# A decode block: softmax in groups between key heads, a fixed VectorE order, and a re-ordered value stage and tail

## Chip, cores, metric

One core of one Trainium2 chip. The metric is device time in microseconds (us). Most quoted times are medians of several executions; a "span" is that of the one profiled execution, from its first to its last instruction, and is 1.7 to 2.1 us shorter than the same execution's time. "Stream" below means the transfers from HBM (the main memory of the chip) into SBUF (the working memory of the core) as a whole. To "evict" a result is to copy it out of the accumulator in which TensorE left it; here VectorE does this.

## The reference, cut to what matters

One token passes an attention block and a feed-forward block, each with a layer norm modulated by a condition `c`. Attention reads the last 4096 keys and values of 32 heads of 192 elements, and each key and value is used once.

```python
mod = (silu(c) @ w_mod)                        # sa, ca, ga, sb, cb, gb: six vectors of 640
h = layernorm(x) * (1 + ca) + sa
q = h @ wq                                     # 32 heads x 192
p = softmax(q @ k.T * 192 ** -0.5)             # per head, 4096 keys
x = x + ga * ((p @ v) @ wo)
h = layernorm(x) * (1 + cb) + sb
x = x + gb * (mish(h @ w1 + b1) @ w2)
```

K and V are 50.3 MB each; with the weights the kernel reads 125.24 MB.

## The kernel before

All large transfers come from one queue (SyncE). K heads, V heads and the weights of the second half share a pool `kv` of six buffers, so a transfer is issued only when the buffer of six tiles earlier is free. For K, VectorE multiplies a head by the query, TensorE adds up the products in twelve matmuls with an identity, VectorE reduces the rest.

```python
kv = ctx.enter_context(tc.tile_pool(name="kv", bufs=6))
pp = ctx.enter_context(tc.tile_pool(name="pp", bufs=2))
...
def k_reduce(h):
    nc.vector.tensor_reduce(out=S[:, h, :], in_=accs.pop(h)[:], axis=AX.X, op=ALU.add)
...
for h in range(H):                                  # K stage; wo comes in six pieces between
    ...
    kt = kv.tile([P, T, Dh], BF, tag="kv")
    nc.sync.dma_start(out=kt[:], in_=A_k_cache[0, h, Sk - W:Sk, :].rearrange("(p t) d -> p t d", p=P))
    ...                                             # at h == 2: both later parts of w_mod
    nc.vector.tensor_tensor(out=prod[:], in0=kt[:], in1=qbc[:, h:h + 1, :].to_broadcast([P, T, Dh]), op=ALU.mult)
    for d1 in range(ND1):
        nc.tensor.matmul(acc[:], lhsT=ident[:], rhs=prod[:, :, d1 * D2:(d1 + 1) * D2], ...)
    accs[h] = acc
    if h >= 1:
        k_reduce(h - 1)
k_reduce(H - 1)

m1 = ...                                            # one softmax for all 32 heads: maximum,
...                                                 # transpose, subtract, Exp, sum, reciprocal
nc.vector.tensor_tensor(out=Pm[:], in0=E[:], in1=rinv[:].unsqueeze(2).to_broadcast([P, H, T]), op=ALU.mult)

for i in range(NPAIR):                              # V stage, two heads at a time
    for hh in range(2):
        nc.sync.dma_start(out=vt[:], in_=A_v_cache[0, h, Sk - W:Sk, :].rearrange("(p t) d -> p (t d)", p=P))
        for t0 in range(0, T, G):
            nc.tensor.matmul(acc[:], lhsT=Pm[:, h, t0:t0 + G], rhs=vt[:, t0 * Dh:(t0 + G) * Dh], ...)
        nc.vector.tensor_copy(out=osb[:, :, hh, :], in_=acc[:])
    ...                                             # six tiny matmuls transpose osb into pt, copied to oT
    if i >= 1:
        wo_stage(i - 1)                             # fifteen matmuls with wo, added to attn
... # loads of w1 (two pieces) and w2 (two pieces), last wo_stage, norm, ph = w1 part, mish, py = w2 part, out
```

Of the kernel before, what the change touches and what calls it, by code (L numbers as in the profile page):

```python
# [7 lines left out]
BF = mybir.dt.bfloat16  # L8
F32 = mybir.dt.float32
ALU = mybir.AluOpType  # L10
AX = mybir.AxisListType
ACT = mybir.ActivationFunctionType
# [4 lines left out]
def kernel(  # L17
# [15 lines left out]
    nc = tc.nc  # L33
    P = 128
    D = A_x.shape[2]
# [5 lines left out]
    KC = D // P  # L41
# [46 lines left out]
    onesf = const.tile([P, P], F32)  # L88
    nc.gpsimd.memset(onesf[:], 1.0)
    epsb = const.tile([P, 1], F32)  # L90
    nc.gpsimd.memset(epsb[:], EPS)
# [71 lines left out]

    S = const.tile([P, H, T], F32)
    modB = const.tile([P, 4 * KC], F32)
    accs = {}

    def k_reduce(h):
        nc.vector.tensor_reduce(out=S[:, h, :], in_=accs.pop(h)[:], axis=AX.X, op=ALU.add)  # L169

# [4 lines left out]
    MODB_AT = 2  # L175
    wmbs = []
    for h in range(H):
        if h in WO_AT:
            b_ = WO_AT[h]
            nc.sync.dma_start(out=wo_t[:, b_ * JB:(b_ + 1) * JB, :],  # L180
                              in_=A_wo[b_ * JB * P:(b_ + 1) * JB * P, :].rearrange("(j p) n -> p j n", p=P))
        kt = kv.tile([P, T, Dh], BF, tag="kv")
        nc.sync.dma_start(out=kt[:], in_=A_k_cache[0, h, Sk - W:Sk, :].rearrange("(p t) d -> p t d", p=P))
        if h == MODB_AT:
            for b_ in range(2):
                wmb = kv.tile([P, KC, 2 * D], BF, tag="kv")
                nc.sync.dma_start(out=wmb[:], in_=w_mod[:, (2 + 2 * b_) * D:(4 + 2 * b_) * D].rearrange("(k p) n -> p k n", p=P))
                wmbs.append(wmb)
        prod = pp.tile([P, T, Dh], BF, tag="prod")
        nc.vector.tensor_tensor(out=prod[:], in0=kt[:], in1=qbc[:, h:h + 1, :].to_broadcast([P, T, Dh]),  # L190
                                op=ALU.mult)
        acc = psA.tile([P, T, D2], F32, tag="A")
        for d1 in range(ND1):
            nc.tensor.matmul(acc[:], lhsT=ident[:], rhs=prod[:, :, d1 * D2:(d1 + 1) * D2],  # L194
                             start=(d1 == 0), stop=(d1 == ND1 - 1))
        accs[h] = acc
        if h >= 1:
            k_reduce(h - 1)
        if h == MODB_AT + 1:
            pmb = psC.tile([P, 4 * KC], F32, tag="C")  # L200
            for j in range(4 * KC):
                wmb = wmbs[j // (2 * KC)]
                jo = (j % (2 * KC)) * P
                for k in range(KC):
                    nc.tensor.matmul(pmb[:, j:j + 1], lhsT=wmb[:, k, jo:jo + P], rhs=scT[:, k:k + 1],
                                     start=(k == 0), stop=(k == KC - 1))
            nc.scalar.copy(out=modB[:], in_=pmb[:])
    k_reduce(H - 1)

    m1 = small.tile([P, H], F32)  # L210
    nc.vector.tensor_reduce(out=m1[:], in_=S[:], axis=AX.X, op=ALU.max)  # L211
    pmT = psC.tile([H, P], F32, tag="C")
    nc.tensor.transpose(pmT[:], m1[:], identf[:])
    gm = small.tile([H, 1], F32)
    nc.vector.tensor_reduce(out=gm[:], in_=pmT[:], axis=AX.X, op=ALU.max)
    dg = small.tile([H, H], F32)
    nc.vector.tensor_scalar_mul(out=dg[:], in0=identf[0:H, 0:H], scalar1=gm[:])
    pgb = psC.tile([P, H], F32, tag="C")
    nc.tensor.matmul(pgb[:], lhsT=onesf[0:H, :], rhs=dg[:], start=True, stop=True)
    nc.vector.tensor_tensor(out=S[:], in0=S[:], in1=pgb[:].unsqueeze(2).to_broadcast([P, H, T]),  # L220
                            op=ALU.subtract)
    E = const.tile([P, H, T], F32)
    nc.scalar.activation(out=E[:], in_=S[:], func=ACT.Exp, scale=SCALE)  # L223
    rs = small.tile([P, H], F32)
    nc.vector.tensor_reduce(out=rs[:], in_=E[:], axis=AX.X, op=ALU.add)  # L225
    pss = psC.tile([P, H], F32, tag="C")
    nc.tensor.matmul(pss[:], lhsT=onesf[:], rhs=rs[:], start=True, stop=True)
    rinv = small.tile([P, H], F32)
    nc.vector.reciprocal(out=rinv[:], in_=pss[:])
    Pm = const.tile([P, H, T], BF)  # L230
    nc.vector.tensor_tensor(out=Pm[:], in0=E[:], in1=rinv[:].unsqueeze(2).to_broadcast([P, H, T]),  # L231
                            op=ALU.mult)

    attn = const.tile([P, KC], F32)
    oTs = {}

    def wo_stage(i):
        oT = oTs.pop(i)
        pa = psC.tile([P, KC], F32, tag="C")
        for n in range(KC):  # L240
            for ci in range(3):
                nc.tensor.matmul(pa[:, n:n + 1], lhsT=wo_t[:, 3 * i + ci, n * P:(n + 1) * P],  # L242
                                 rhs=oT[:, ci:ci + 1], start=(ci == 0), stop=(ci == 2))
        if i == 0:
            nc.vector.tensor_copy(out=attn[:], in_=pa[:])
        else:
            nc.vector.tensor_tensor(out=attn[:], in0=attn[:], in1=pa[:], op=ALU.add)  # L247

    G = 2
    for i in range(NPAIR):  # L250
        osb = small.tile([G, G, 2, Dh], BF, tag="osb")
        for hh in range(2):
            h = 2 * i + hh
            vt = kv.tile([P, T * Dh], BF, tag="kv")
            nc.sync.dma_start(out=vt[:], in_=A_v_cache[0, h, Sk - W:Sk, :].rearrange("(p t) d -> p (t d)", p=P))
            acc = psB.tile([G, G, Dh], F32, tag="B")
            for t0 in range(0, T, G):
                nc.tensor.matmul(acc[:], lhsT=Pm[:, h, t0:t0 + G], rhs=vt[:, t0 * Dh:(t0 + G) * Dh],  # L258
                                 start=(t0 == 0), stop=(t0 == T - G))
            nc.vector.tensor_copy(out=osb[:, :, hh, :], in_=acc[:])  # L260
        pt = psC.tile([P, 3], F32, tag="C")
        for ci in range(3):
            for g in range(G):
                nc.tensor.matmul(pt[:, ci:ci + 1],  # L264
                                 lhsT=osb[:, g].rearrange("k a d -> k (a d)")[:, ci * P:(ci + 1) * P],
                                 rhs=ident[0:G, g:g + 1], start=(g == 0), stop=(g == G - 1))
        oT = small.tile([P, 3], BF, tag="oT")
        nc.vector.tensor_copy(out=oT[:], in_=pt[:])  # L268
        oTs[i] = oT
        if i >= 1:  # L270
            wo_stage(i - 1)
    w1a = kv.tile([P, 3, F], BF, tag="kv")
# [4 lines left out]
    for b_ in range(2):  # L277
        w = kv.tile([P, FC // 2, D], BF, tag="kv")
        nc.sync.dma_start(out=w[:], in_=B_w2[b_ * (F // 2):(b_ + 1) * (F // 2), :].rearrange("(f p) n -> p f n", p=P))
        w2_t.append(w)  # L280
    wo_stage(NPAIR - 1)

    x1 = const.tile([P, KC], F32)
    nc.vector.tensor_tensor(out=x1[:], in0=attn[:], in1=modB[:, 0:KC], op=ALU.mult)
    nc.vector.tensor_tensor(out=x1[:], in0=x1[:], in1=xT[:], op=ALU.add)
    xn2 = layernorm_T(x1[:], "l2")
    h2a = small.tile([P, KC], F32)
    nc.vector.scalar_tensor_tensor(out=h2a[:], in0=modB[:, 2 * KC:3 * KC], scalar=1.0, in1=xn2[:],
                                   op0=ALU.add, op1=ALU.mult)
    h2T = small.tile([P, KC], BF)  # L290
    nc.vector.tensor_tensor(out=h2T[:], in0=h2a[:], in1=modB[:, KC:2 * KC], op=ALU.add)  # L291

    ph = psC.tile([P, FC], F32, tag="C")
    nc.tensor.matmul(ph[:], lhsT=ident[:], rhs=b1T, start=True, stop=False)
    for f in range(FC):
        for k in range(KC):
            wt = w1a[:, k, f * P:(f + 1) * P] if k < 3 else w1b[:, k - 3, f * P:(f + 1) * P]
            nc.tensor.matmul(ph[:, f:f + 1], lhsT=wt, rhs=h2T[:, k:k + 1],  # L298
                             start=False, stop=(f == FC - 1 and k == KC - 1))
    hc = small.tile([P, FC], F32)  # L300
    nc.vector.tensor_scalar(out=hc[:], in0=ph[:], scalar1=20.0, scalar2=-80.0, op0=ALU.min, op1=ALU.max)
    u = small.tile([P, FC], F32)
# [7 lines left out]
    actT = small.tile([P, FC], BF)  # L310
    nc.vector.tensor_tensor(out=actT[:], in0=nn_[:], in1=ph[:], op=ALU.mult)

    py = psC.tile([P, KC], F32, tag="C")
    for n in range(KC):
        for f in range(FC):
            wt = w2_t[f // (FC // 2)]
            nc.tensor.matmul(py[:, n:n + 1], lhsT=wt[:, f % (FC // 2), n * P:(n + 1) * P], rhs=actT[:, f:f + 1],  # L317
                             start=(f == 0), stop=(f == FC - 1))
    x2 = small.tile([P, KC], F32)
    nc.vector.tensor_tensor(out=x2[:], in0=py[:], in1=modB[:, 3 * KC:4 * KC], op=ALU.mult)  # L320
    x2b = small.tile([P, KC], BF)
    nc.vector.tensor_tensor(out=x2b[:], in0=x2[:], in1=x1[:], op=ALU.add)
    pxo = psC.tile([KC, P], BF, tag="C")
    nc.tensor.transpose(pxo[:], x2b[:], ident[:])
    xo = small.tile([KC, P], BF)
# [32 lines left out]
```

## Time and profile before

| | before |
|---|---|
| time, median of 16 executions (lowest to highest) | 334.83 us (330.14 to 336.43) |
| profiled execution, and its span | 335.64, 333.9 us |
| DMA bytes, mean rate over the span | 125.47 MB, 376 GB/s |
| PE (TensorE), DVE (VectorE), ACT (ScalarE) busy | 70%, 49%, 2% |

At the time of the prediction the first four of these executions were known (median 335.51). Two of the sixteen are near 330.1 and the rest above 333; the profiled one lies near the median.

How to read it: the DMA row gives the busy tenths of the transfer engines in 40 slices, the row under it the GB/s. In a table of windows a line is a stretch of time with the busy time of PE, PE weight loads, DVE, ACT, POOL (counts of instructions in brackets), then TensorE's granted clock (as a share of full speed), the DMA share and GB/s. In a line of waits the three numbers are the idle time in all, how often, and the longest. In a timeline a line is start, length, engine, source line, operation, result<-inputs, and in square brackets how long the engine stood idle before and what ended that. The lines themselves are in the prediction.

### The profile page before, as it was taken

What the parts mean: (1) busy time and instruction counts of PE and PEld (TensorE: products, weight loads), DVE (VectorE), ACT (ScalarE), POOL (GpSimd) and SP (SyncE); (2) the same over time, 40 slices, a digit from 0 to 9 for tenths busy, and PEclk for the clock granted to TensorE, in tenths of its full rate; (3) what the DMA queues carried; (4) which work ended last, traced back from release to release, by engine and by line L of the source; (5) the groups of instructions that cost most, each with busy time, mean ns of one, the idle gap of its engine ahead of it and who ended that gap; (6) DMA issues with size and microseconds to landing.
All of it is one profiled execution on the core that took longest, in us unless ns stands there. A gap on an engine that the chain in (4) does not pass through costs nothing.

```text
span 333.9 us, 3612 instructions
## 1 busy us (share of the span) xinstructions
PE 234.8 (70%) x1572; PEld 110.1 (33%) x1574; DVE 164.8 (49%) x179; ACT 7.4 (2%) x15; POOL 1.3 (0%) x10
## 2 busy tenths in 40 slices
PE   0495684587587586675774928997888878888844
PEld 0342251233233132232231313554444444443423
DVE  1222858589787887797797552212111121112231
ACT  1021000000000000000000010000000000000000
POOL 1000000000000000000000000000000000000000
PEclk9999795879989699699599675999999999999985
DMA  7999999999999999999999950999999999999900
GB/s 271 410 410 428 403 420 398 427 417 410 424 396 428 425 399 428 413 407 428 399 426 427 425 229 16 402 430 428 423 423 425 425 429 423 424 422 410 304 0 2
DMA packets 21702, 125.47 MB, mean 376 GB/s; under 512 B 1335, under 2 KB 9015, under 8 KB 13495
## 3 DMA queue, kind: packets, MB, share of 16 engines
q1 hardware_dynamic: 21642, 125.25, 91.8%
q8 instruction: 12, 0.20, 0.2%
q14 instruction: 4, 0.02, 0.0%
q10 hardware_dynamic: 44, 0.01, 0.0%
HBM read 125.24 MB, written 0.00 MB: 375 GB/s over the span
## 4 chain that ended last, share of the span: by engine, by line
PE 49%; DVE 29%; DMA 15%; issue 6%; ACT 1%; SPq 0%; DVEq 0%
PE acc L258 27%; DVE prod L190 19%; PE acc L194 16%; DMA kt<-in_A_k_cache_dram 10%; DMA wq_t<-in_A_wq_dram 5%; DVE osb L260 5%; DVE S L169 2%; PE pa L242 2%; PE pt L264 2%; PE py L317 1%; PE ph L298 1%; DVE Pm L231 0%; DVE S L220 0%; DVE m L211 0%; DVE rs L225 0%
## 5 line engine op out<-in xcount | busy, mean ns | idle before, releaser
L194 PE MATMUL acc<-prod,ident 128*128 128x512 bf16 x384 | 106.2, 439 | 51.1 <-DVE prod L190 51.1
L190 DVE TENSOR_TENSOR prod<-kt,qbc 128x6144 bf16<-128x6144 bf16 x32 | 106.6, 3350 | 3.2 <-DMA kt<-in_A_k_cache_dram 3.2
L258 PE MATMUL acc<-vt,Pm 128*2 128x384 bf16 x512 | 90.8, 332 | 1.7 <-DVE Pm L231 1.7
L194 PEld LDWEIGHTS <-ident 128*128 128x128 bf16 x384 | 42.0, 109 | 115.0 <-issue 83.9
L260 DVE CAST osb<-acc 2x384 bf16<-2x384 f32 x32 | 17.5, 546 | 80.9 <-PE acc L258 80.9
L258 PEld LDWEIGHTS <-Pm 128*2 128x2 bf16 x512 | 41.1, 85 | 39.7 <-issue 3.1
L169 DVE TENSOR_REDUCE S<-acc 128x32 f32<-128x512 f32 x32 | 22.0, 688 | 31.2 <-PE acc L194 31.2
L157 PE MATMUL pq<-wq_t,hrep 128*128 128x512 bf16 x58 | 15.6, 428 | 6.6 <-DMA wq_t<-in_A_wq_dram 6.3
L264 PE MATMUL pt<-ident,osb 2*128 2x1 bf16 x96 | 7.1, 163 | 16.7 <-DVE osb L260 16.6
L264 PEld LDWEIGHTS <-osb 2*128 2x128 bf16 x96 | 4.3, 92 | 28.8 <-DVE osb L260 27.3
L162 DVE CAST qbc<-pq 128x512 bf16<-128x512 f32 x6 | 4.2, 692 | 17.3 <-PE pq L157 17.3
L157 PEld LDWEIGHTS <-hrep 128*128 128x128 bf16 x60 | 6.4, 108 | 15.4 <-issue 5.7
L242 PE MATMUL pa<-oT,wo_t 128*128 128x1 bf16 x240 | 8.4, 164 | 0.3 <-DVE oT L268 0.3
L247 DVE TENSOR_TENSOR attn<-attn,pa 128x5 f32<-128x5 f32 x15 | 2.4, 161 | 10.4 <-PE pa L242 10.4
L242 PEld LDWEIGHTS <-wo_t 128*128 128x128 bf16 x240 | 7.1, 96 | 0.6 <-issue 0.2
L268 DVE CAST oT<-pt 128x3 bf16<-128x3 f32 x16 | 2.6, 165 | 6.0 <-PE pt L264 5.9
L117 PE MATMUL pvT<-ident,rows 22*128 22x22 bf16 x1 | 0.2, 174 | 7.0 <-DMA rows<-in_B_b_dram 7.0
L223 ACT ACTIVATE E<-S 128x1024 f32<-128x1024 f32 x1 | 1.1, 1056 | 146.7 <-DVE S L220 146.7
L160 ACT CAST qbc<-pq 128x512 bf16<-128x512 f32 x6 | 3.5, 586 | 18.4 <-PE pq L157 18.4
L119 DVE COPY vecT<-pvT 128x22 bf16<-128x22 bf16 x1 | 0.2, 169 | 7.2 <-PE pvT L117 7.2
L108 ACT ACTIVATE lnv<-var,epsb 128x1 f32<-128x1 f32 x2 | 0.6, 294 | 127.8 <-DVE var L106 127.8
L298 PE MATMUL ph<-h2T,w1a 128*128 128x1 bf16 x36 | 1.7, 165 | 2.3 <-DVE h2T L291 2.3
(77 smaller groups left out, 38.6 us busy)
## 6 DMA issues: line engine op xcount, KB each, us to landing
kt<-in_A_k_cache_dram SPq DMA_DIRECT2D x32, 1536.0 KB, 19.2
vt<-in_A_v_cache_dram SPq DMA_DIRECT2D x32, 1536.0 KB, 10.6
wq_t<-in_A_wq_dram SPq DMA_DIRECT2D x3, 2560.0 KB, 18.8
wo_t<-in_A_wo_dram SPq DMA_DIRECT2D x6, 1280.0 KB, 20.7
wmb<-in_w_mod_dram SPq DMA_DIRECT2D x2, 1600.0 KB
w<-in_B_w_dram SPq DMA_DIRECT2D x2, 960.0 KB
wma<-in_w_mod_dram SPq DMA_DIRECT2D x1, 1600.0 KB, 7.0
w1a<-in_B_w_dram SPq DMA_DIRECT2D x1, 1152.0 KB, 9.1
```

The costliest lines, as they stand in the source:

```text
L157: nc.tensor.matmul(pq[:], lhsT=hrep[:, k, :], rhs=wq_t[:, k, n * 512:(n + 1) * 512], start=(k == 0), stop=(k == KC - 1))
L160: nc.scalar.copy(out=qflat[:, n * 512:(n + 1) * 512], in_=pq[:])
L162: nc.vector.tensor_copy(out=qflat[:, n * 512:(n + 1) * 512], in_=pq[:])
L169: nc.vector.tensor_reduce(out=S[:, h, :], in_=accs.pop(h)[:], axis=AX.X, op=ALU.add)
L190: nc.vector.tensor_tensor(out=prod[:], in0=kt[:], in1=qbc[:, h:h + 1, :].to_broadcast([P, T, Dh]), op=ALU.mult)
L194: nc.tensor.matmul(acc[:], lhsT=ident[:], rhs=prod[:, :, d1 * D2:(d1 + 1) * D2], start=(d1 == 0), stop=(d1 == ND1 - 1))
L242: nc.tensor.matmul(pa[:, n:n + 1], lhsT=wo_t[:, 3 * i + ci, n * P:(n + 1) * P], rhs=oT[:, ci:ci + 1], start=(ci == 0), stop=(ci == 2))
L258: nc.tensor.matmul(acc[:], lhsT=Pm[:, h, t0:t0 + G], rhs=vt[:, t0 * Dh:(t0 + G) * Dh], start=(t0 == 0), stop=(t0 == T - G))
L260: nc.vector.tensor_copy(out=osb[:, :, hh, :], in_=acc[:])
L264: nc.tensor.matmul(pt[:, ci:ci + 1], lhsT=osb[:, g].rearrange("k a d -> k (a d)")[:, ci * P:(ci + 1) * P], rhs=ident[0:G, g:g + 1], start= ...
L298: nc.tensor.matmul(ph[:, f:f + 1], lhsT=wt, rhs=h2T[:, k:k + 1], start=False, stop=(f == FC - 1 and k == KC - 1))
L317: nc.tensor.matmul(py[:, n:n + 1], lhsT=wt[:, f % (FC // 2), n * P:(n + 1) * P], rhs=actT[:, f:f + 1], start=(f == 0), stop=(f == FC - 1))
```

## The change

Its intent: take the softmax chain out of the way of the V stage by doing heads 0 to 7, 8 to 15, 16 to 23 between later K heads; fix VectorE's order in the K stage (product of head h+1, then the reduce of head h); take stalls out of TensorE's V stage (transposes behind the next head's matmuls, normalisation folded into the eviction, `wo` on VectorE for 14 of 16 pairs); move the last third of `w_mod` behind V; and shorten the tail's chain. The core of the diff:

```diff
     def k_reduce(h):
-        nc.vector.tensor_reduce(out=S[:, h, :], ...)
+        with tc.issue_after(prods[min(h + 1, H - 1)].ins):
+            reds[h] = nc.vector.tensor_reduce(out=S[:, h, :], ...)
+    GH = 8
+    def softmax_steps(g):          # four steps for heads g*8 .. g*8+7
+        s1: max over the free axis, transpose          s2: max, diagonal, matmul broadcast
+        s3: negm on ScalarE, then per head
+            nc.scalar.activation(out=Pm[:, h_, :], in_=S[:, h_, :], func=ACT.Exp, scale=SCALE,
+                                 bias=negm[:, j:j + 1], accum_out=rs[:, h_:h_ + 1])
+        s4: matmul with ones over rs, reciprocal into rinv
...
-            for b_ in range(2): ... wmb ...            # both later parts of w_mod in the K stage
+            wmb1 = kv.tile(...)                        # one of them
-        nc.vector.tensor_tensor(out=prod[:], ...)
+        with tc.issue_after(reds[h - 2].ins) if h >= 2 else nullcontext():
+            prods[h] = nc.vector.tensor_tensor(out=prod[:], ...)
+        if pending:
+            pending.pop(0)()
+            if h % GH == 0:
+                pending.extend(softmax_steps(h // GH - 1))
...                                                    # V stage
-            nc.vector.tensor_copy(out=osb[:, :, hh, :], in_=acc[:])
-        pt = ... transposes ...; wo_stage(i - 1)
+            nc.vector.tensor_scalar_mul(out=osb[:, :, hh, :], in0=acc[:], scalar1=rinv[0:G, h:h + 1])
+            if hh == 0 and i >= 1:
+                with tc.issue_after(last.ins):
+                    pts[i - 1] = transposes(osbs.pop(i - 1))
+                wo_dve(i - 1)                          # three scalar_tensor_tensor; the last two pairs: wo_pe
...                                                    # the last V pair is loaded in halves
+    wmb2 = kv.tile(...); nc.sync.dma_start(out=wmb2[:], in_=w_mod[:, 4 * D:6 * D]...)   # behind V
...                                                    # tail: norm folded into two columns of ph, sums by accum_out,
                                                       # the residual added inside the last matmul
```

## The prediction

> **What bounds the kernel now.** I read the 40-slice view first, then a table of windows, then the waits and the timeline at the places where the DMA row falls off.
>
> ```profile
> DMA  7999999999999999999999950999999999999900
> GB/s 271 410 410 428 403 420 398 427 417 410 424 396 428 425 399 428 413 407 428 399 426 427 425 229 16 402 430 428 423 423 425 425 429 423 424 422 410 304 0 2
> ```
>
> A slice is 8.35 us. The DMA engines are full almost everywhere, at 400 to 430 GB/s, so the memory stream is the bound. It is broken twice: about slices 23 and 24, and at the end. The kernel reads 125.24 MB. The windows (microseconds from the start; the last two columns are the DMA share and GB/s) say how long it is broken:
>
> ```profile
> 0.00:196.00 196.00, 127.13 (x598) 53.31 (x600) 134.56 (x91) 5.68 (x11) 1.27 (x10) 0.88 1.01 410
> 198.00:207.00 9.00, 5.74 (x19) 2.50 (x20) 2.80 (x3) 0.24 (x1) 0.00 (x0) 0.50 0.00 0
> 225.00:300.00 75.00, 62.20 (x528) 32.01 (x527) 14.18 (x40) 0.00 (x0) 0.00 (x0) 1.00 1.01 424
> 316.00:317.00 1.00, 0.36 (x10) 0.29 (x10) 0.55 (x1) 0.00 (x0) 0.00 (x0) 1.00 0.94 343
> 317.00:318.00 1.00, 1.00 (x20) 0.67 (x17) 0.16 (x1) 0.00 (x0) 0.00 (x0) 1.00 0.05 15
> ```
>
> By summing windows, 80.4 MB (all K, weights so far, and exactly six V heads, one per buffer of the pool) have landed by 196.4; then nothing moves until 208.2: a **hole of 11.8 us**. The last byte of all comes at 317.05, so the end of 333.9 lies **16.9 us** behind it. The timeline shows the cause of the hole:
>
> ```profile
> 192.44 0.69 DVE L169 TENSOR_REDUCE S<-acc 128x32 f32<-128x512 f32 x1 [2.32 <-PE acc L194]
> 200.61 1.22 DVE L231 TENSOR_TENSOR Pm<-E,rinv 128x1024 bf16<-128x1024 f32 x1
> 201.89 7.94 PE L258 MATMUL acc<-vt,Pm 128*2 128x384 bf16 x32 [1.71 <-DVE Pm L231]
> ```
>
> The softmax of all 32 heads is a serial chain between the last K reduce and the first V matmul; no V buffer comes free in it. In the V stage the pace is set by TensorE all the same:
>
> ```profile
> SPq L255 <- PE acc L258: 99.4, 26, 19.4
> PE pt L264 <- DVE osb L260: 16.6, 26, 0.6
> 225.90 0.20 PE L264 MATMUL pt<-ident,osb 2*128 2x1 bf16 x2 [0.64 <-DVE osb L260]
> 226.03 0.53 PE L242 MATMUL pa<-oT,wo_t 128*128 128x1 bf16 x15
> ```
>
> The queue that issues V waits on the matmuls that free buffers, and TensorE itself stands 0.64 us per head behind the eviction of its own result. A pair of heads takes 7.57 us (230.06 back to 222.50), 2 x 1.573 MB in that time being 416 GB/s, a little under the 424 the stream still manages by working off a backlog.
>
> **What the Trainium skill says.** "DMA: Bandwidth & Descriptors", section "Where 436 GB/s comes from", gives 435 GB/s as the ceiling of the ports into SBUF and about 358 as the share of HBM for a core. The trace shows 424 to 428, so here the first figure is the near one and no headroom in rate is left. The same page, "Anatomy of one DMA", says that the semaphore waits for the last byte to be confirmed. The trace agrees: 1.638 MB and the first 2.621 MB of wq have passed at about 13.2, and the matmul that waits for them starts at 14.18, so 1.0 us. "Perfetto Trace Analysis", "Optimization Strategy", suggests interleaving regimes that are bound by different engines; the hole is such a border. "ScalarE: Activation LUTs", "What ACT_TABLE_LOAD costs", gives an activation with a pointer bias about 280 ns + 0.833 ns per element; the trace has 294 ns for 128x1 (lnv), so I take 0.31 us for each new 128x32 exponential.
>
> **The change, part by part.** No byte is added or taken. So I follow the stream.
>
> (1) *Softmax in four groups of eight heads.* Three groups go between heads of the K stage. In the instruction order of the changed build, the first V matmul stands directly behind the last K matmul and waits for its DMA alone; the last group's small steps lie between V matmuls. The 11.8 us hole should vanish. Added on VectorE per group: a 128x256 maximum (about a quarter of the 1.22 us, plus overhead, 0.35), gm 0.25, dg 0.2, a reciprocal 0.2: 1.0 us. Removed: four 128x1024 passes of 1.22 us, all from the hole. On ScalarE 8 x 0.31 = 2.5 us per group; in groups 1 and 3 the sum over partitions follows at once on TensorE, which then stands some 3 us. Five buffers ahead, about 18 us, absorb that.
>
> (2) *Fixed order prod(h+1), reduce(h).* Before, VectorE idled 31.2 us in 16 of the reduces, behind TensorE. Two instructions that don't wait repeat each 3.87 us (prod 3.35 and reduce 0.69, overlapped a little). Five heads: 19.4 + 0.6 softmax = 20.0 us. The stream needs 5 x 1.573/0.428 = 18.4 and a wo piece at about 357 GB/s (from the dips to 402) 3.7: 22.1 us. So VectorE keeps up, and K ends with its transfers: 69.3 MB, near 170, + 8 us for the last products. Nothing of this shortens the stream itself; it keeps the backlog small.
>
> (3) *V stage.* Transposes go behind the next head's matmuls, and wo moves to VectorE for 14 pairs. TensorE per pair: 2 x 2.71 + 0.45 = 5.9 us. VectorE: 2 x 0.55 + 0.17 + 3 x 0.82 (estimate: the 128x640 f32 cast took 0.819) = 3.7 us. The stream: 3.146/0.424 = 7.4 us. So the stream sets the pace.
>
> (4) *Second half of the modulation weights moved* from the K stage to behind V: 1.638 MB, 4.0 us at 410. The stream is neutral, but these bytes, which V need not follow, now come after V.
>
> (5) *Tail.* V has to be used while 5.57 MB follow it: 4.0 us + w1 5.1 (1.966 MB at 385, window 306:310) + w2 5.8 (about 340, the 302 of 314:316 over its share 0.88) = 14.9 us.
>
> Stream: by 192.4 (196.4 less 4.0) the same six V heads are in; 26 more are 40.9 MB / 0.426 = 95.9 us: **288.3**. Plus 14.9: last byte at **303.2**. Compute beside it, from the V end: +1.0, half a head 1.4, eviction 0.6, transposes 0.3; pmc waits for its weights until 293.3 and takes 1.45; pa and the shortened norm 2.1: 296.9; ph waits for w1 until 298.4 and takes 1.75; eight VectorE and ScalarE steps 2.0: 302.2. That is before the last weights are usable at 304.2, so the weights decide. Then py 1.75, and from py to the end 3.34 as before (330.56 to 333.9) less one 0.2 step: **309.1** span. Run times stood 1.7 above the span (335.64 against 333.9): **310.8 us**, 25 less, of which the hole gives 11.8, the end (16.9 to 5.9) 11.0, and full rate in place of TensorE's pace and the ragged last transfers some 2.
>
> **The rivals.** *A: TensorE still sets the V stage's pace.* If 7.57 us a pair stayed, V would run from 193 for 121 us to 314, and with the weights loaded beside it some 9 us would follow: 323 + 1.7 = 325 us. For it: the same number of V matmuls, and their clock can be halved (0.50 in 198:207). Against: the stall behind osb is gone, and from 210 on the clock was 1.00. *B: the K stage stays bound by VectorE and TensorE*, since the enforced order and the group steps lie on both in-order queues and the clock there was 0.85. If K ended at 193 again, six V heads would be in and TensorE would free them at 2.75 us each, so little hole returns: 2 to 5 us, 313 to 316. For it: the transfers' landing took 14 us at the end of K against 33.6 at its start, so compute was slower than the stream. Against: idle time that (2) removes. *C: the tail is a chain, not a stream.* Moving wmb2 behind V puts pmc, in order on TensorE, before the last pa; if this or a step I sized too small overruns by 2 to 4 us, 312 to 315. *D: faster*: K and V alone ran at 428 in 170:195; at that rate throughout V, 1 us less, and w1 and w2 queued in time may run at 400: 2.5 us less, 307.
>
> **Range and chances.** D gives 307, B and C together up to 317; A is outside and unlikely. All rivals but A's worst keep more than 2% (below 328.8). Predicted 310.8, range 307 to 317; faster 0.97, same 0.025, slower 0.005.
>
> **What would show it.** Right: a DMA row of nines up to about 303 without a hole; TensorE's V matmuls waiting for DMA vt; the queue's waits shrinking from longest 19.4; K's last reduce near 178; py waiting for w, with 5 to 6 us after the last byte. Wrong: a hole over 2 us at the K to V border (B), no DMA waits of the V matmuls and 3.7 us or more per head on TensorE (A), the last byte well before the start of py (C). If the stream ran below 415 GB/s in V, the size of everything is off.

## The result, and the profile after

The changed kernel takes 306.92 us (306.83 to 307.24 in ten executions) against 334.83: 8% less. The ratio is 0.9204, interval 0.9168 to 0.9239; ratios here are the mean time of one kernel's runs over that of the other's of the same rounds, so not quite the ratio of these medians. Executions over 1.5% slower than the fastest of the same kernel are left out of the means. The time is 3.9 us below the predicted 310.8 and 0.08 below the lower edge of the range.

The slices of the changed kernel, and windows of it (columns as above):

```profile
DMA  7999999999999999999999999999999999999991
GB/s 261 422 421 433 417 438 410 432 427 415 429 415 430 424 412 436 425 411 433 428 414 431 433 428 426 432 429 427 432 432 422 430 435 424 428 433 417 413 397 42
```
```profile
33.00:170.00 137.00, 95.54 (x434) 41.07 (x434) 124.03 (x75) 8.34 (x52) 0.00 (x0) 0.93 1.02 424
225.00:275.00 50.00, 39.05 (x260) 18.97 (x259) 27.51 (x42) 0.00 (x0) 0.00 (x0) 1.00 1.01 429
```

There is no hole. In the first window the kernel before moved 414 GB/s, here 424. The border between K and V, from the timeline:

```profile
174.80 1.46 PE L318 MATMUL acc<-vt,Pm 128*2 128x384 bf16 x8
174.91 0.69 DVE L178 TENSOR_REDUCE S<-acc 128x32 f32<-128x512 f32 x1 [2.24 <-PE acc L237]
175.63 0.42 DVE L188 TENSOR_REDUCE m<-S 128x8 f32<-128x256 f32 x1
176.19 0.27 PE L190 MATMUL pmT<-identf,m 128*8 128x128 f32 x1
```

The first V matmuls start before the last K reduce, 27 us earlier than before (201.89), and the last group's softmax steps lie among them. Now the waits of the V stage, and one pair of it:

```profile
PE acc L318 <- DMA vt<-in_A_v_cache_dram: 19.0, 25, 1.0
```
```profile
226.65 0.14 DVE L269 COPY oTf<-pt 128x3 f32<-128x3 f32 x1
226.83 2.73 DVE L274 SCALAR_TENSOR_TENSOR acc_wo<-wo_t,oTf,acc_wo 128x640 f32<-128x640 bf16 x3
226.97 2.76 PE L318 MATMUL acc<-vt,Pm 128*2 128x384 bf16 x16 [0.66 <-DMA vt<-in_A_v_cache_dram]
```

TensorE waits for V data, 25 times and at most 1.0 us: the stream is the pace. VectorE's share of `wo` lies under it. And the end:

```profile
291.70 0.60 DVE L320 TENSOR_SCALAR osb<-acc,rinv 2x384 bf16<-2x384 f32 x1 [2.55 <-PE acc L318]
299.91 0.30 PE L419 MATMUL py<-actT,w 128*128 128x1 bf16 x6 [2.23 <-DVE actT L413]
300.61 1.60 PE L419 MATMUL py<-actT,w 128*128 128x1 bf16 x54 [0.39 <-DMA w<-in_B_w_dram]
```

`py` first waits for the compute chain (actT, 299.9) and then 0.39 us for the last piece of w2: chain and stream arrive almost together.

The best comparison of the two traces is by bytes, since both move the same. I summed the GB/s of 2 us windows (this counts 0.2 MB of instruction fetches too). The predicted column is from the prediction's sum. The last column belongs to a run explained below.

| MB moved | before | predicted | changed | changed, buffers 64 bytes higher |
|---|---|---|---|---|
| 78.77 | 192.3 us | 192.4 | 188.5 | 192.2 |
| 119.67 | 300.8 | 288.3 | 284.0 | 288.7 |
| 125.2 (as good as all) | 316.5 | 303.2 | 297.9 | 303.4 |
| end of span | 333.9 | 309.1 | 305.2 | 310.8 |

By the differences of the columns "before" and "changed": of the 28.7 us of span, 3.8 come while the first 78.77 MB move (in the changed kernel these are all that stands ahead of V, and six V heads), 13.0 from the border and the V stage, 1.8 from the last transfers, 10.1 from the part behind the last byte. The 3.8 were not in my prediction at all.

### The profile page after: what moved, and what is told of

The parts are those of the page before. It is cut to its first block, busy times and chain, and to the rows that moved or that the text cites. A ratio compares the mean times of both kernels' runs of the same rounds, so it can differ in the third digit from the quotient of the medians.

```text
span 305.2 us, 3330 instructions
## 1 busy us (share of the span) xinstructions
PE 219.5 (72%) x1388; PEld 104.1 (34%) x1390; DVE 197.3 (65%) x221; ACT 17.4 (6%) x83; POOL 1.4 (0%) x11
## 4 chain that ended last, share of the span: by engine, by line
DMA 45%; PE 24%; DVE 23%; issue 5%; ACT 3%; SPq 0%; DVEq 0%
DMA vt<-in_A_v_cache_dram 25%; DVE prod L233 19%; PE acc L237 11%; PE acc L318 9%; DMA wq_t<-in_A_wq_dram 8%; DMA kt<-in_A_k_cache_dram 7%; DMA w<-in_B_w_dram 4%; ACT Pm L205 3%; DVE S L178 3%; PE pq L159 1%; DVE acc_wo L274 1%; PE py L419 1%; PE pr L280 0%; PE pmb L250 0%; PE pss L210 0%
## 5 line engine op out<-in xcount | busy, mean ns | idle before, releaser
L237 PE MATMUL acc<-prod,ident 128*128 128x512 bf16 x384 | 96.1, 406 | 37.1 <-DVE prod L233 37.1
L237 PEld LDWEIGHTS <-ident 128*128 128x128 bf16 x384 | 39.6, 104 | 91.7 <-issue 55.3
L320 DVE TENSOR_SCALAR osb<-acc,rinv 2x384 bf16<-2x384 f32 x32 | 19.3, 604 | 51.9 <-PE acc L318 51.9
L274 DVE SCALAR_TENSOR_TENSOR acc_wo<-wo_t,oTf,acc_wo 128x640 f32<-128x640 bf16 x41 | 36.3, 885 | 1.5
L205 ACT ACTIVATE Pm<-S,negm 128x32 bf16<-128x32 f32 x32 | 9.8, 308 | 0.1
L205 ACT ACTIVATION_READ_ACCUMULATOR Pm<-S,negm 128x1 f32 x32 | 6.0, 186 | 0.0
L210 PE MATMUL pss<-rs,onesf 128*128 128x8 f32 x8 | 1.4, 254 | 6.2 <-ACT Pm L205 6.2
L301 PEld LDWEIGHTS <-osb 2*128 2x128 bf16 x96 | 3.4, 91 | 6.4 <-issue 5.3
L301 PE MATMUL pt<-ident,osb 2*128 2x1 bf16 x96 | 4.9, 161 | 0.7 <-DVE osb L320 0.7
L419 PE MATMUL py<-actT,w 128*128 128x1 bf16 x60 | 1.9, 165 | 2.6 <-DVE actT L413 2.2
```

The source lines that it names most:

```text
L205: nc.scalar.activation(out=Pm[:, h_, :], in_=S[:, h_, :], func=ACT.Exp, scale=SCALE, bias=negm[:, j:j + 1], accum_out=rs[:, h_:h_ + 1])
L274: nc.vector.scalar_tensor_tensor(out=acc_wo[:], in0=wo_t[:, 3 * i + ci, :], scalar=oTf[:, ci:ci + 1], in1=acc_wo[:], op0=ALU.mult, op1=ALU ...
L301: nc.tensor.matmul(pt[:, ci:ci + 1], lhsT=osb[:, g].rearrange("k a d -> k (a d)")[:, ci * P:(ci + 1) * P], rhs=ident[0:G, g:g + 1], start= ...
L320: nc.vector.tensor_scalar_mul(out=osb[:, :, hh, :], in0=acc[:], scalar1=rinv[0:G, h:h + 1])
L419: nc.tensor.matmul(py[:, n:n + 1], lhsT=wt[:, f % (FC // 2), n * P:(n + 1) * P], rhs=actT[:, f:f + 1], start=(f == 0), stop=(f == FC - 1))
```

## The experiments

Twelve kernels ran; all gave correct results, and each was timed against the kernel before in the same rounds. "e" runs undo a part of the change; "a" runs move addresses.

| run | median us | ratio to before (interval) | GB/s, 10 to 20 us | start of streamed buffers modulo 256 |
|---|---|---|---|---|
| changed | 306.92 | 0.9204 (0.9168 to 0.9239) | 422 | 0 |
| e1_block_softmax | 314.45 | 0.9407 (0.9365 to 0.9449) | 410 | 64 |
| e2_free_order | 312.80 | 0.9349 (0.9319 to 0.9379) | 421 | 0 |
| e3_block_softmax_free_order | 326.00 | 0.976 (0.9705 to 0.9816) | 411 | 64 |
| e4_old_v_order | 315.01 | 0.9415 (0.9389 to 0.9442) | 410 | 192 |
| a1_before_aligned | 333.67 | 0.9985 (0.9919 to 1.005) | 421 | 0 |
| a2_after_shift64 | 312.49 | 0.9357 (0.93 to 0.9414) | 409 | 64 |
| e1a_block_softmax_aligned | 309.26 | 0.9245 (0.9173 to 0.9318) | 420 | 0 |
| e4a_old_v_aligned | 311.30 | 0.9321 (0.9264 to 0.9379) | 422 | 0 |
| e3a_both_aligned | 325.27 | 0.969 (0.9635 to 0.9745) | 421 | 0 |
| e5_wmb2_early | 310.96 | 0.9269 (0.9229 to 0.9309) | 422 | 0 |
| a3_after_shift128 | 312.50 | 0.9328 (0.9297 to 0.936) | 411 | 128 |
| e6_wo_rows | 305.63 | 0.9122 (0.9092 to 0.9153) | 422 | 0 |

### First four: parts undone

**e1_block_softmax**, the softmax of before in place of the groups:

```diff
-            if h % GH == 0:
-                pending.extend(softmax_steps(h // GH - 1))
-    for f_ in pending + softmax_steps(H // GH - 1):
-        f_()
+    m1 = ...; E = ...; Pm = E * rinv          # the block of the kernel before
-            nc.vector.tensor_scalar_mul(out=osb[:, :, hh, :], in0=acc[:], scalar1=rinv[0:G, h:h + 1])
+            nc.vector.tensor_copy(out=osb[:, :, hh, :], in_=acc[:])
```

> The changed kernel with the softmax of the kernel before (all 32 heads in one chain after the last K reduce); all else stays changed. Theory P (my prediction: the hole of 11.8 us is the softmax chain, and splitting it is what closes it): the hole comes back, DMA row shows about 11 us of zeros near 188 to 200, time about 318 us. Rival Q (a hole needs six full V buffers before the first V matmul ends; the fixed K order already ends K at 175, the chain of 9.5 us then ends near 185, before the stream has filled six buffers at about 188 to 192): no hole over 2 us, time 307 to 309 us.

Measured: 314.45, between the two. **e2_free_order**, the fixed order taken out:

```diff
-        with tc.issue_after(prods[min(h + 1, H - 1)].ins):
+        with nullcontext():
-        with tc.issue_after(reds[h - 2].ins) if h >= 2 else nullcontext():
+        with nullcontext():
```

> The changed kernel without the fixed order of products and reduces in the K stage (the scheduler's own order, as before); the split softmax stays. Theory P (the order does nothing to the stream): 307 us, K stream at 424 GB/s. Rival Q (K compute ends near 188 to 193 again, and the stream in K falls back from 424 to about 416 GB/s, 69.3 MB near 170 in place of 166.5): 309 to 313 us, a hole of 0 to 4 us.

Measured: 312.80. The last K reduce starts at 190.16 in place of 174.91, and the stream has pauses near 183 and 193, as Q says:

```profile
190.16 0.69 DVE L178 TENSOR_REDUCE S<-acc 128x32 f32<-128x512 f32 x1 [1.90 <-PE acc L237]
```
```profile
182.00:184.00 2.00, 1.64 (x4) 0.56 (x4) 2.00 (x2) 0.00 (x0) 0.00 (x0) 0.50 0.64 147
192.00:194.00 2.00, 2.00 (x13) 1.02 (x12) 0.70 (x3) 1.16 (x8) 0.00 (x0) 1.00 0.00 0
```

But the K stream kept its 424 GB/s, against Q's second half. **e3_block_softmax_free_order**, both edits:

> Both undone: one softmax chain and the free K order. P and Q both expect the hole back, 8 to 12 us of zeros in the DMA row, and 317 to 321 us. If this costs far more than the sum of the two single undoings, the two parts cover for each other (Q). If it costs no more than the one-chain softmax alone, P.

Measured: 326.00, with the hole back, but 5 us above the expected range. **e4_old_v_order**, the V loop of before (transposes behind their pair, `wo_pe` for all pairs) with the new tail:

```diff
-            if hh == 0 and i >= 1:
-                with tc.issue_after(last.ins):
-                    pts[i - 1] = transposes(osbs.pop(i - 1))
-                ...wo_dve / wo_pe...
+        pts[i] = transposes(osb)
+        if i >= 1:
+            wo_add(i - 1)                     # wo_pe, times ga, added to base
```

> The V stage as before: transposes right behind their pair, wo on TensorE for all pairs; all else changed. If TensorE's 7.57 us per pair comes back as the pace: V from 175 for 121 us, last V matmul near 296 in place of 292, then the same chain: 309 to 311 us, no or few waits for vt. If the stream alone sets the end (backlog from the earlier K end covers it): 307 us.

Measured: 315.01, above the expectation. Of these four only e2 came out where one of my theories had put it. What stood out was the stream: e1, e3 and e4 moved the *first* weights, which no edit touches, as slowly as the kernel before (410 GB/s from 10 to 20 us), while e2 and the changed kernel moved them at 421 to 422. Whatever makes the difference acts before any changed instruction of the K stage runs. The edits do add and remove small tiles, and these lie ahead of the large buffers in SBUF. In the built programs `wq_t` starts at byte 49088 of each partition before (192 modulo 256) and at 47872 in the changed kernel (0 modulo 256), and the `kv` buffers, `prod` and `wo_t` follow in steps that are multiples of 256: the changed kernel and e2 have all starts at multiples of 256, the four others do not.

### Addresses

**a1_before_aligned** and **a2_after_shift64** are the kernel before and the changed kernel with one line each:

```diff
     const = ctx.enter_context(tc.tile_pool(name="const", bufs=1))
+    shift = const.tile([128, 32], BF)         # 64 bytes per partition, never used
```

> The kernel before with one unused 64-byte tile ahead of its constants, so that every streamed SBUF buffer starts 64 bytes higher, at a multiple of 256 bytes. Nothing else. Theory A (the stream's rate hangs on the start address: the two traces so far with starts at multiples of 256 moved wq at 421 GB/s in 10 to 20 us, the four with other starts at 410, whatever else was in them): wq at 421, K stream near 424, the wo pieces' dips at about 380 in place of 360; since K and V in this kernel are paced in part by TensorE and the hole stays, 330 to 333 us. Rival B (the rate comes from the changed order or depth of the queue): wq at 410, time unchanged, 335.

> The changed kernel with the same unused 64-byte tile, so that its buffers start at 64 modulo 128 as in the kernel before. Theory A: wq falls to 410, K stream to about 415, last byte about 4 to 5 us later, time 310.5 to 312.5 (which is what I had predicted for the change at the old rates, 310.8). Rival B: no change, 306.9.

The windows of 10 to 20 us of the kernel before, of a1, of the changed kernel and of a2, in this order:

```profile
10.00:20.00 10.00, 6.00 (x31) 2.49 (x29) 2.13 (x5) 0.79 (x2) 0.00 (x0) 1.00 1.03 410
```
```profile
10.00:20.00 10.00, 6.18 (x22) 2.51 (x22) 2.00 (x5) 1.17 (x2) 0.00 (x0) 1.00 1.02 421
```
```profile
10.00:20.00 10.00, 6.17 (x20) 2.44 (x19) 2.07 (x5) 0.73 (x2) 0.00 (x0) 1.00 1.03 422
```
```profile
10.00:20.00 10.00, 6.08 (x29) 2.58 (x28) 2.13 (x5) 1.05 (x3) 0.00 (x0) 1.00 1.02 409
```

The DMA share is the same, the bytes are not. A 64-byte tile that nobody uses costs the changed kernel 5.6 us (312.49 against 306.92; the intervals of the ratios do not touch) and switches the rate in both kernels. In the kernel before the faster rate is worth nothing clear (0.9985, interval over 1): its stream reaches 78.77 MB at 188.3 in place of 192.3, and then stands in a longer hole, because there compute sets the pace (its first V matmul starts at 200.41, before it was 201.89). I had expected 330 to 333; it took 333.67, since what the stream gains ahead of the hole it loses in it.

The DMA records of the traces also say how the time is lost. A packet here is one contiguous row of a transfer. The mean packet of 1280 bytes (`wo`, w2) took 55.1 ns in the changed kernel and 59.5 in a2, one of 4096 bytes (`wq`) 159.3 and 163.8, one of 12288 bytes (K, V) 460.6 and 465.2. So each packet takes some 3 to 5 ns more, whatever its length, and transfers of short rows lose most. Summed over all packets of a row and divided by 16 engines that is 5.7 us, as much as the difference in time. And the end of a2, to set beside that of the changed kernel above:

```profile
306.20 1.60 PE L420 MATMUL py<-actT,w 128*128 128x1 bf16 x54 [1.22 <-DMA w<-in_B_w_dram]
```

**a3_after_shift128** (`[128, 64]` in the same line):

> The changed kernel with an unused tile of 128 bytes: starts at 128 modulo 256. If a multiple of 128 is enough: 306.9 us, wq at 421 GB/s. If it takes 256: 312.5 us as with 64 bytes, wq at 410.

Measured 312.50: a multiple of 128 is not enough; of the starts tried (0, 64, 128, 192 modulo 256) only 0 gives the higher rate. The other three cost the same: a packet of 1280 bytes took 59.5 ns in a2 (64), 59.3 in a3 (128) and 59.4 in e4 (192).

### The parts again, at equal addresses

**e1a_block_softmax_aligned** and **e4a_old_v_aligned** are e1 and e4 with a tile of 192 and 64 bytes:

> The one-chain softmax again, now with buffers at multiples of 256 (pad of 192 bytes), so that it differs from the changed kernel in the softmax alone. Theory A: of the 7.5 us measured without the alignment some 4 to 5 were the address; 309.5 to 311, with a hole of 2 to 4 us (six V buffers full near 188.5 to 190, first V matmuls done near 188 to 193 at a halved clock). If the address does nothing: 314.4 again.

> The old V stage again with buffers at multiples of 256 (pad of 64 bytes). Theory A: some 4 of the 8.1 us were the address; 309 to 311.5, what is left being TensorE's 7.57 us per pair against the stream's 7.3. If the address does nothing: 315.0 again.

Measured 309.26 (just under the expected range) and 311.30. So 5.2 of e1's 7.5 us and 3.7 of e4's 8.1 were the address. What is left of e1 is 2.3 us (by the medians; the intervals of the ratios overlap, though its four runs, 307.75 to 310.16, all lie above the changed kernel's ten). Its first V eviction starts at 190.0, and the stream dips to 135 and 111 GB/s in two windows of 2 us near 190: a short hole, as expected:

```profile
188.00:190.00 2.00, 2.00 (x9) 0.77 (x7) 0.00 (x0) 0.00 (x0) 0.00 (x0) 0.53 0.32 135
190.00:192.00 2.00, 2.00 (x14) 1.06 (x13) 0.55 (x1) 0.00 (x0) 0.00 (x0) 1.00 0.58 111
```

In e4a the stream is that of the changed kernel to within 0.2 us (119.67 MB at 284.0, 125.2 at 297.9), so the V stage's stalls never reach it. They show only at the end; compare with the changed kernel's 291.70 and 299.91 above:

```profile
296.27 0.60 DVE L330 TENSOR_SCALAR osb<-acc,rinv 2x384 bf16<-2x384 f32 x1 [2.33 <-PE acc L328]
304.44 1.74 PE L418 MATMUL py<-actT,w 128*128 128x1 bf16 x60 [2.22 <-DVE actT L412]
```

The last V head is evicted 4.6 us later, `py` starts 4.5 us later, and the time is 4.4 us longer. The tail is a chain again: `py` starts 6.5 us after 125.2 MB have passed.

**e3a_both_aligned**, both K-stage parts undone (e3 with a tile of 192 bytes):

> One-chain softmax and free K order together, buffers at multiples of 256 bytes, so that it differs from the changed kernel in these two alone. With the address out of the way, single undoings cost 2.3 us (softmax, 309.3) and 5.9 us (order, 312.8). If the two cover for each other, both together cost more than 8.2: a hole of 12 to 14 us, since the stream fills six V buffers by 188.5 while the first V matmul ends near 207; 319 to 322 us. If they simply add: 315.

Measured 325.27: 18.4 us above the changed kernel, more than the expected 319 to 322 and far more than 2.3 and 5.9 together. Its slices, and its border:

```profile
DMA  7999999999999999999999870499999999999992
```
```profile
191.47 0.69 DVE L179 TENSOR_REDUCE S<-acc 128x32 f32<-128x512 f32 x1 [2.04 <-PE acc L238]
200.92 10.40 PE L336 MATMUL acc<-vt,Pm 128*2 128x384 bf16 x48 [1.71 <-DVE Pm L271]
```

This is the border of the kernel before to within a microsecond (192.44 and 201.89 there). The address matters little here, 0.7 us between e3 and e3a: again the stream does not set the pace.

### The place of the last modulation weights

**e5_wmb2_early**: the load of `wmb2` and its 50 matmuls back to the third head of the K stage.

```diff
             wmb1 = kv.tile(...); dma_start(wmb1 ...)
+            wmb2 = kv.tile(...); dma_start(wmb2 ...)
...
-    wmb2 = kv.tile(...); dma_start(wmb2 ...)          # behind V
```

> The last 1.638 MB of modulation weights back in the K stage, their matmuls too; all else changed, addresses as in the changed kernel. Theory P (the chain behind the last V head decides): V lands 4 us later, the chain is 1.4 us shorter without these matmuls: 308.5 to 309.5 us. Rival Q (TensorE was late with the last two V heads anyway, ending them at 291.7 where their data were in by about 285, and the last weights decide): 306.5 to 307.5. In both the last byte stays near 298.

Measured 310.96, 4.0 us longer, with the last bytes where they were (125.2 MB at 297.8). In its trace:

```profile
297.26 0.60 DVE L328 TENSOR_SCALAR osb<-acc,rinv 2x384 bf16<-2x384 f32 x1 [2.55 <-PE acc L326]
304.44 1.74 PE L419 MATMUL py<-actT,w 128*128 128x1 bf16 x60 [2.23 <-DVE actT L413]
```

The last V head is evicted 5.6 us later than in the changed kernel, and the chain behind it is about 1 us shorter. So P, though the time is 1.5 us above its range: in the changed kernel 4 us of stream that V does not need were hidden behind the chain.

### A version that beats both

**e6_wo_rows**: `wo` read in runs of three rows, eight transfers.

```diff
-    NWO = 6;  WO_AT = {5 * (b + 1): b for b in range(NWO)}
+    NWO = 8;  WO_AT = {5 + 3 * b: b for b in range(NWO)}
-        in_=A_wo[...].rearrange("(j p) n -> p j n", p=P)
+        in_=A_wo[...].rearrange("(i p c) n -> p i c n", p=P, c=3)
-        lhsT=osb[:, g].rearrange("k a d -> k (a d)")[:, ci * P:(ci + 1) * P]
+        lhsT=osb[:, g].rearrange("k a d -> k (a d)").rearrange("k (p c) -> k p c", c=3)[:, :, ci]
```

> A version that may beat both: the changed kernel with wo laid out so that a partition reads three rows together (3840 contiguous bytes in place of 1280), in eight transfers of two pairs each; the transposes take every third column. The wo pieces now move at about 390 GB/s by the K stage's bytes (29.3 MB in 69.2 us with K at 432); at 430, 7.86 MB take 1.9 us less: 304.5 to 305.5 us, dips to 370 to 385 gone. If the row length does not matter: 306.9.

Measured 305.63 (305.43 to 305.72), just above the expected range and 1.3 us less than the changed kernel; its four runs lie below all ten of that kernel, though in other rounds. From 33 to 170 us it moved 428 GB/s where the changed kernel moved 424. Row length and the number of transfers changed together, so the time does not say which of them did it. The packets speak for the row length: one of 3840 bytes took 149.0 ns on average, three of 1280 bytes in the changed kernel 165. No run separates the two.

## Why the prediction was right, and where not

- **The bound.** Right: with no hole left, the stream sets the end, TensorE waits for `vt`, and `py` for the last weights.
- **The sum.** My stream ran at the rates of the kernel before, and a2, the changed kernel at such addresses, follows it to within 0.4 us at 78.77, 119.67 and 125.2 MB (table above). The changed kernel itself is ahead by 3.9, 4.3 and 5.3 us. The term that was mis-sized is the rate: I took 410 to 416 GB/s in K and 340 to 385 for w1 and w2 as the stream's own, and they were those of buffers that do not start at multiples of 256. "No headroom in rate is left" was wrong for the same reason: from 33 to 170 us the changed kernel moves 424 GB/s in place of 414. That its buffers start at multiples of 256 is luck: it follows from the sum of the small tiles' sizes, and neither the diff nor the prediction shows anything of it.
- **Behind the last byte.** "+1.0" for the last weights to be usable was too small: in a2 `py` can take them at 306.2, where 125.2 MB had passed at 303.4; in the changed kernel it is 300.6 after 297.9. The bytes of the last transfer come in thinly (155 GB/s in the changed kernel from 298 to 299 us, 50 in the next), so the 1.0 us measured with more transfers behind it did not carry over. (The section of the skill that I cited for it describes transfers issued by GpSimd; these come from SyncE.) This error of 1.7 us hid a part of the other.
- **Part (1).** "The 11.8 us hole should vanish" was right, but the softmax was only half of the cause. With the K order fixed, one undivided chain costs only 2.3 us, since K then ends near 175 us, some 14 us before the stream has filled six V buffers (78.77 MB near 189 in e1a).
- **Part (2).** "Nothing of this shortens the stream itself; it keeps the backlog small" is the step that fell. The free order costs 5.9 us in e2 even with the split softmax. K then ends near 190, when all six buffers are taken, and the stream stops. Each of the two parts removes most of the hole alone; without both it costs 18.4 us. Giving the hole to the softmax was an allotment that a single trace could not support.
- **Part (3), and rival A.** The stream hides the old V stage wholly (e4a), so A's 325 was far too high: I had let V start at 193, as before. What the new order gives is 4.4 us at the end. The estimate of 0.82 us for the `wo` steps was 0.885 in the trace and cost nothing.
- **Parts (4) and (5).** "The stream is neutral" was right, and that the weights behind V buy time was only implied; e5 puts it at 4.0 us. In the changed kernel chain and stream end within 0.7 us of each other; I had put 2.0 between them (302.2 and 304.2). The chain was undersized at its head: the eviction of the last V head should have started 2.4 us after the last V byte ("+1.0", "half a head 1.4") and started 7.7 us after it (291.70, 284.0). The trace shows TensorE from 280.9 to 282.1 on the ten matmuls that add up VectorE's share of `wo`, and then its clock at 0.50 to 0.53 until 285; no run separates the two. Only a part of the 5.3 us counts: in a2 `pmc` (the matmuls with the moved modulation weights), which follows, still waited 0.20 us for its weights.
- **Rivals B and C.** B did not occur: the three stops of TensorE behind the group sums took up to 2.8 us each, as sized, without a mark on the stream. C is what e4a and e5 look like.
- **Rival D** named the time that was measured, 307, but mostly by luck. Its two gains came to 0.4 us (V at 428 GB/s, 95.5 us in place of 95.9; D had 1.0) and 1.0 us (the last 5.5 MB at 398 GB/s, 13.9 us in place of 14.9; D had 2.5). The 3.9 us gained by 78.77 MB are not in it, nor is the error of 1.7 us that took a part back.
- **What stays open.** Why the start address sets the rate, and whether all or only some of the streamed buffers must be aligned. The runs show that it does, at which starts, and that it costs time by the packet; the unused tile moves the constants and small tiles too. No run undoes the shortened tail of part (5) or the halved last loads alone, so their share of the 10.1 us behind the last byte is not measured.

## What to carry to other kernels

When a transfer stream sets the time, ask of every stall whether it lasts longer than the buffers ahead: the undivided softmax cost 2.3 us or 12.5 (18.4 less 5.9), depending on when the stage before it ended. Undo parts singly and together before giving a gain to one of them. And before comparing two variants of a stream-bound kernel compare the rate of a transfer that neither touches, and look at the start addresses of the buffers: here 64 unused bytes cost 5.6 us, more than three of the four parts that were undone singly (2.3, 4.4, 4.0 and 5.9).

## What the Trainium skill lacked or had wrong

- "DMA: Bandwidth & Descriptors", section "How a descriptor splits into AXI transactions", says that transactions start at multiples of 256 bytes and that a start in between costs extra beats, and speaks of reads. The page has no figure for the SBUF side of a load. Here only addresses in SBUF moved, and 64, 128 or 192 modulo 256 in place of 0 took the first weights from 420 to 422 GB/s down to 409 to 411, and the stream-bound kernel from 306.9 to 312.5 us. A packet took 3 to 5 ns more, the same for all three starts. That the page's splitting is the mechanism, no run here shows.
- The same page, "Where 436 GB/s comes from", says without a condition that the HBM side (about 358) binds for transfers between HBM and SBUF, although the same section calls a measurement of its own (425 for 16 MB) near the other ceiling. Here, with one core at work, 424 to 429 GB/s were held for 50 us and more, so 358 did not bind.
- "VectorE: DVE Perf Modes", in its table of rates, has no row for `scalar_tensor_tensor`. Here 128x640 ones with a bf16 first input and the f32 accumulator as second took 885 ns on average (41 of them), and the single `tensor_scalar` without the accumulator 552 ns.
